# Scores and AV of two tiles of a fused attention and MLP kernel on the diagonal quadrants of TensorE, V kept by parity halves, and the first part of w_in in four transfers

## The chip, the core and the metric

The kernel runs on one core of one Trainium2 chip. The metric is the device time of one execution in microseconds, as the median of several runs. Lower is better. The core's engines are TensorE (PE, with its weight loads shown apart as PEld), VectorE (DVE), ScalarE (ACT), GpSimd (POOL) and SyncE (SP), which here only issues DMA transfers. Each engine works through its own list in order.

## The reference, cut to what matters

```python
q, k, v: (8, 8, 576, 64) float32     # batch, heads, sequence, head dimension
# attention within chunks of 64 keys, no mixing between chunks
scores = 1/8 * q_c @ k_c^T           # per batch, head and chunk: 64 x 64
attn   = softmax(scores)
x      = (attn @ v_c) as (4608, 512) # tokens by heads x head dimension
h      = gelu(x @ w_in)              # w_in: 512 x 2048
out    = h @ w_out                   # w_out: 2048 x 512
```

## The kernel before, in words

**Tiles.** The 4608 tokens are cut into nine tiles of 512 tokens: tile t < 8 holds the first eight chunks of batch t, and tile 8 holds the ninth chunk of all eight batches. Two heads stand together on the 128 partitions, as a pair `g` of four: head 2g on partitions 0 to 63, head 2g+1 on 64 to 127. `CT` = 8 is the number of chunks of a tile, `CH` = 64 their length, `MT` = 512.

**Attention of tiles 0 and 1** (the later seven go another way, by `quad_S` and `quad_av`, which use 64x64 products on all four quadrants of TensorE). Q and K are cast to bf16 and turned by TensorE (`transposed`, L207); `att_Tq` (L213) copies the turned Q, `att_Tk` (L220) the turned K. K's copy goes into `k_bds[g]`, in which each chunk is a 128x128 block with the two heads on its diagonal and zeros beside them. `att_S` (L361 to 369) makes eight products of 128x128 weights by 64 columns for a pair of heads, one for each chunk (L366), and the exponential (L368). V is loaded with 128 keys on the partitions (`load_v`, L181) and cast into `v_bds[i]`, which again holds diagonal blocks (`cast_v`, L201: one piece for each head and parity of the chunk, 64x256 each). `att_av` makes eight products for a pair (L440) and multiplies by the inverse sums into `x` (L442). The zeros beside the diagonals are set by `zero_k` and `zero_v` (L71 to 77) and by two memsets in the main list (L1172).

**The MLP of tile 0** runs while the weights arrive. For each block `f` of 128 of the 2048 hidden columns, four products (one for each part `ks` of the 512) and a GELU (L465 by `by_halves`, called at L481 and L491; L484, L493). `by_halves` cuts a product of 512 columns into two of 256. Blocks 0 and 1 are done first, part by part (`mm1_slices`, L1203). The second layer of tile 0 goes by rows of `w_out` (`mm2_rows`, L1025, f = 0 to 11, four products each), the last four rows by `mm2_slot` (L989).

**What sets the order.** The program is a list written by hand from L1098 on. `phase(0, {...})` at L1204 hangs the attention of tile 1 between the rows of tile 0's second layer: key s of the table names what is issued ahead of row s. So the scores of tile 1's pairs are issued ahead of rows 8, 9, 10 and 11, and its AV products ahead of the later slots 13, 14 and 15 and, for the last pair, in tile 1's first layer (`last_av`).

**Transfers.** SP issues all loads in one list: Q and K of tile 0 in pieces, V of tile 0 (eight transfers, one for each head), `w_in` in four parts of 1 MB (the first three in two transfers each, L1067, of 256 columns; the fourth in one), the four parts of `w_out` (L1075, 1 MB each) with Q and K of tile 1 between them, V of tile 1. Arrivals are in float32 in one of six `arrival` buffers; `win[c](i, engine)` (L1070) and `wout[c](i, engine)` (L1078) cast a block of them to bf16. Row f = 8 of the second layer, L1025, needs the first block of `w_out`'s third part, which POOL casts (L1186).

Of the kernel before, what the change touches and what calls it, by code (L numbers as in the profile page):

```python
# [11 lines left out]
def kernel(  # L12
# [10 lines left out]
    P = 128  # L23
# [46 lines left out]

    def zero_v(i, eng):  # L71
        eng.memset(v_bds[i][0:CH, :, :, CH:P], 0.0)
        eng.memset(v_bds[i][CH:P, :, :, 0:CH], 0.0)

    def zero_k(k_bd, eng):
        eng.memset(k_bd[0:CH, :, CH:P], 0.0)
        eng.memset(k_bd[CH:P, :, 0:CH], 0.0)
# [99 lines left out]
    def load_v(t):  # L177

        tiles[t]["vf"] = stage_tile()[:].rearrange("p (h n d) -> p h n d", h=H, d=D)
        for h in range(H):  # L180
            nc.sync.dma_start(tiles[t]["vf"][:, h], v[t, h, 0:MT, :].rearrange("(n key) d -> key n d", key=P))  # L181
# [16 lines left out]
    def cast_v(t, g, r, copies):  # L198
        to = slice(CH * r, CH * (r + 1))
        for c, copy in enumerate(copies):  # L200
            copy(v_bds[t % NV][to, c:CT:2, g, to], tiles[t]["vf"][CH * c:CH * (c + 1), 2 * g + r])  # L201
# [14 lines left out]
    def att_Tk(t, g, copy):  # L216
        tp = transposed(t, "k", g)
        for r in range(2):
            sl = slice(CH * r, CH * (r + 1))
            copy(k_bds[g][sl, :, sl].rearrange("p i (c j) -> p i c j", j=J), tp[sl])  # L220
# [139 lines left out]

    def att_S(t, g):  # L361
        st = tiles[t]
        pool, tag = (ps_tp, "tp") if t == 1 and g > 1 else (ps_at, "at")
        s_ps = pool.tile([P, CT, CH], f32, tag=tag, name="s_ps")
        for i in range(CT):
            nc.tensor.matmul(s_ps[:, i, :], k_bds[g][:, i, :], st["qT", g][:, i], start=True, stop=True)  # L366
        pT = work.tile([P, CT, CH], bf16, tag="pT", name="pT", bufs=5)
        nc.scalar.activation(pT[:], s_ps[:], Act.Exp, scale=scale)  # L368
        st["pT", g] = pT
# [65 lines left out]
    def att_av(t, g):  # L435
        st = tiles[t]
        pool, tag = (ps_tp, "tp") if t == 1 and g > 1 else (ps_at, "at")
        av_ps = pool.tile([P, CT, CH], f32, tag=tag, name="av_ps")
        for i in range(CT):
            nc.tensor.matmul(av_ps[:, i, :], v_bds[t % NV][:, i, g, :], st["pT", g][:, i, :], start=True, stop=True)  # L440
        x, av, rc = st["x"][:, g, :], av_ps[:].rearrange("p i e -> p (i e)"), st["rc", g][:]
        nc.vector.tensor_tensor(x, av, rc.rearrange("p n e -> p (n e)"), op=mybir.AluOpType.mult)  # L442
# [17 lines left out]
    def by_halves(to, left, right, start, stop):  # L460

        n = to.shape[-1] // 2
        for a in range(2):
            cols = slice(n * a, n * (a + 1))
            nc.tensor.matmul(to[:, cols], left, right[:, cols], start=(start and a == 0), stop=stop, skip_group_check=True)  # L465

    def mm1_slices(t, pools, steps):
# [4 lines left out]
        for step in steps:  # L472
# [3 lines left out]
            for ks in step[1]:  # L476
                for f in step[0]:
                    if ks == 0:
                        pool, tag = pools[f]
                        h_ps[f] = pool.tile([P, MT], f32, tag=tag, name="h_ps")  # L480
                    (nc.tensor.matmul if t else by_halves)(h_ps[f][:], w_in_sb[:, ks, f * P:(f + 1) * P], st["x"][:, ks, :],  # L481
                                                           start=(ks == 0), stop=(ks == KS - 1))
                    if ks == KS - 1:
                        nc.scalar.activation(st["h"][:, f, :], h_ps[f][:], Act.Gelu)  # L484

    def mm1_slot(t, f):
# [3 lines left out]
        for ks in range(KS):  # L490
            (nc.tensor.matmul if t else by_halves)(h_ps[:], w_in_sb[:, ks, f * P:(f + 1) * P], tiles[t]["x"][:, ks, :],  # L491
# [520 lines left out]
    def mm2_rows(t, f):  # L1012
# [8 lines left out]
        for ms, fi in order:  # L1021
# [3 lines left out]
            (by_halves if 2 <= f < 5 else nc.tensor.matmul)(  # L1025
# [71 lines left out]
    with tc.manual_schedule():  # L1097
# [4 lines left out]
        win = [load_w_in(c, 2) for c in range(NWC - 1)]  # L1102
        act_table(Act.Exp)
        keep_warm(7)
        zero_k(k_bds[0], nc.gpsimd)
        zero_k(k_bds[1], nc.gpsimd)
        zero_v(0, nc.vector)
        T, S_, U, A = att_units(0, DV, AC)
        cast_qk(0, "k", 0, PO)
        zero_k(k_bds[2], nc.gpsimd)  # L1110
        cast_qk(0, "k", 1, PO)
        zero_k(k_bds[3], nc.gpsimd)
        cast_qk(0, "k", 2, PO)
        cast_qk(0, "k", 3, PO)
        for g in range(G - 1):
            for r in range(2):
                cast_v(0, g, r, (PO, PO))
        cast_v(0, G - 1, 0, (PO, PO))
        win[0](0, PO)
# [29 lines left out]
        cast_v(0, G - 1, 1, (DV, DV))  # L1149
        A[2]()  # L1150
        win[0](1, AC)
# [4 lines left out]
        win[0](2, DV)  # L1156
# [3 lines left out]
        for c in range(1, NWC):  # L1160
# [8 lines left out]
            if c < 3:  # L1169
                r = slice(CH * (c - 1), CH * c)  # L1170
                o = slice(CH * (2 - c), CH * (3 - c))
                nc.gpsimd.memset(v_bds[1][r, :, :, o], 0.0)  # L1172
# [16 lines left out]
        for g in (0, 2, 3):  # L1189
            for r in range(2):  # L1190
                cast_v(1, g, r, (PO, PO))
# [7 lines left out]
        def sums():  # L1199
# [3 lines left out]
        mm1_slices(0, (mm, mm), (((0, 1), range(KS)),))  # L1203
# [3 lines left out]
                      11: [lambda: wout[3](3, AC), S_[3]], 12: [lambda: cast_v(1, 1, 0, (AC, AC)), lambda: cast_v(1, 1, 1, (AC, AC)), sums],  # L1207
                      13: [A[0], lambda: over[0](2), lambda: over[0](3), U[1]], 14: [A[1], U[2]], 15: [A[2], U[3]]},
              by_rows=True, first=2)
# [158 lines left out]
```

## Time and profile before

| | us |
|---|---|
| median of 3 runs | 267.13 |
| lowest, highest | 266.97, 267.51 |
| the profiled execution | 267.09 |
| its span in the trace | 265.5 |
| PE busy | 256.1 (96% of the span) |
| DVE, ACT, POOL busy | 223.1, 190.5, 103.2 |

The span begins at the first instruction of the program in the trace; 1.6 us of the profiled execution lie around it. All times of places below are from the span's start. The chain of waits is followed back from the last instruction: at each step to what released it, or to the instruction before it on its engine. "PEld" rows are weight loads, which run beside the products. "SPq" is the sequencer of SP, which issues transfers.

### The profile page before, as it was taken

How to read it: one execution, taken by the hardware profiler on the slowest of the kernel's cores; microseconds unless marked ns; L12 is line 12 of the kernel's file. 1: busy time of each engine (PE TensorE's matmuls, PEld its weight loads, DVE VectorE, ACT ScalarE, POOL GpSimd, SP SyncE). 2: the span in 40 equal slices, each digit the busy share in tenths (PEclk: the TensorE clock that was granted, in tenths of full speed). 3: DMA queues.
4: the chain of work that ended last, by engine and by line, in shares of the span. 5: the costliest groups of instructions: out<-in, count | busy, mean ns of one | idle time of the engine just before them, and what ended most of it. 6: DMA issues, size and time to landing. Idle time of an engine off the chain costs nothing.

```text
span 265.5 us, 7854 instructions
## 1 busy us (share of the span) xinstructions
PE 256.1 (96%) x3122; PEld 210.6 (79%) x3122; DVE 223.1 (84%) x394; ACT 190.5 (72%) x386; POOL 103.2 (39%) x225
## 2 busy tenths in 40 slices
PE   6789999999999999999999999999999999999993
PEld 2478875556888888887888888888888888888882
DVE  6874986898897599678999999999999999948772
ACT  3856758987767987898888588947894789227720
POOL 7767778702364291481372095009411300000000
PEclk9999999999999999999999999999999999999998
DMA  6999998999979979999999988998973410130014
GB/s 201 268 311 396 395 401 236 283 193 289 243 195 284 220 175 244 275 239 249 276 245 232 267 186 237 217 175 195 264 160 80 134 42 2 41 119 3 2 40 125
DMA packets 123416, 54.02 MB, mean 203 GB/s; under 512 B 97776, under 2 KB 120304, under 8 KB 123376
## 3 DMA queue, kind: packets, MB, share of 16 engines
q1 hardware_dynamic: 123072, 53.23, 77.4%
q8 instruction: 25, 0.41, 0.7%
q10 hardware_dynamic: 304, 0.26, 0.3%
q14 instruction: 15, 0.12, 0.1%
HBM read 36.70 MB, written 9.44 MB: 174 GB/s over the span
## 4 chain that ended last, share of the span: by engine, by line
PE 76%; DMA 10%; ACT 7%; SPq 4%; issue 1%; DVE 0%; POOL 0%
PE hs_ps L601 31%; PE y_ps L761 22%; PE y_ps L791 13%; DMA arrival<-in_moe_w_out_dram 8%; ACT h L609 3%; SPq L181 2%; PE h_ps L491 2%; DMA arrival<-in_moe_w_in_dram 2%; PE av_ps L349 2%; PE h_ps L481 2%; ACT pT L272 2%; SPq L142 1%; PE y_ps L1025 1%; PE y_ps L989 1%; PE s_ps L264 1%; ACT L1095 1%
## 5 line engine op out<-in xcount | busy, mean ns | idle before, releaser
L609 ACT ACTIVATE h<-hs_ps 128x512 bf16<-128x512 f32 x87 | 49.6, 609 | 6.5 <-PE hs_ps L601 5.7
L238 POOL CAST v_nat<-arrival 128x256 bf16<-128x256 f32 x56 | 24.9, 473 | 33.5 <-DMA arrival<-in_v_dram 23.1
L601 PEld LDWEIGHTS <-w_in_sb 128*128 128x128 bf16 x348 | 33.9, 98 | 4.7 <-issue 0.2
L194 POOL CAST q_nat<-arrival 128x256 bf16<-128x256 f32 x40 | 16.8, 467 | 50.2 <-DMA arrival<-in_k_dram 25.3
L601 PE MATMUL hs_ps<-x,w_in_sb 128*128 128x256 bf16 x232 | 31.8, 272 | 0.0
L761 PEld LDWEIGHTS <-h 128*128 128x128 bf16 x240 | 23.2, 98 | 2.8
L1095 ACT ACT_TABLE_LOAD x16 | 20.5, 1283 | 1.3 <-PEq L1352 1.0
L190 POOL CAST k_nat<-arrival 128x256 bf16<-128x256 f32 (+1 forms) x44 | 19.1, 476 | 5.3 <-DMA arrival<-in_k_dram 5.3
L721 ACT COPY kept<-y_ps 128x512 f32<-128x512 f32 (+1 forms) x17 | 9.0, 536 | 16.0 <-PE y_ps L761 15.9
L761 PE MATMUL y_ps<-w_out_sb,h 128*128 128x256 bf16 x160 | 18.6, 273 | 0.0
L761 PE MATMUL y_ps<-v_bd,k_bd 128*128 128x256 bf16 x160 | 18.5, 273 | 0.1
L761 PEld LDWEIGHTS <-k_bd 128*128 128x128 bf16 x160 | 15.6, 98 | 2.1 <-issue 0.2
L618 ACT COPY hs_ps<-hs_ps 128x512 f32<-128x512 f32 x29 | 16.2, 583 | 0.6 <-PE hs_ps L601 0.5
L601 PE MATMUL hs_ps<-k_bd,w_in_sb 128*128 128x256 bf16 x116 | 16.6, 272 | 0.0
L493 ACT ACTIVATE h<-h_ps 128x512 bf16<-128x512 f32 x21 | 12.5, 604 | 5.5 <-PE h_ps L465 4.1
L272 ACT ACTIVATE pT<-s_ps 128x512 bf16<-128x512 f32 x28 | 14.4, 599 | 1.8 <-PE s_ps L264 1.8
L791 PEld LDWEIGHTS <-h 128*128 128x128 bf16 x144 | 13.8, 98 | 1.7
L465 PE MATMUL h_ps<-x,w_in_sb 128*128 128x256 bf16 x128 | 14.5, 273 | 0.1
L601 PE MATMUL hs_ps<-k_bd,w_in_more 128*128 128x256 bf16 x96 | 14.2, 273 | 0.0
L601 PEld LDWEIGHTS <-w_in_more 128*128 128x128 bf16 x128 | 12.5, 98 | 2.0 <-issue 0.3
L726 DVE TENSOR_TENSOR kept<-y_ps,kept 128x512 f32<-128x512 f32 (+1 forms) x16 | 10.4, 651 | 4.3 <-PE y_ps L761 2.3
L465 PEld LDWEIGHTS <-w_in_sb 128*128 128x128 bf16 x128 | 12.3, 98 | 2.1 <-DVE w_in_sb L1070 0.7
(175 smaller groups left out, 638.9 us busy)
## 6 DMA issues: line engine op xcount, KB each, us to landing
arrival<-in_v_dram SPq DMA_DIRECT2D x58, 128.0 KB, 3.2
arrival<-in_k_dram SPq DMA_DIRECT2D x28, 256.0 KB, 5.6
arrival<-in_q_dram SPq DMA_DIRECT2D x7, 1024.0 KB, 6.9
out_dram<-kept SPq DMA_DIRECT2D x24, 256.0 KB, 3.2
arrival<-in_moe_w_out_dram SPq DMA_DIRECT2D x4, 1024.0 KB, 12.1
arrival<-in_moe_w_in_dram SPq DMA_DIRECT2D x6, 512.0 KB, 8.5
out_dram<-y_sb SPq DMA_DIRECT2D x8, 256.0 KB, 2.5
arrival<-in_v_dram SPq DMA_DIRECT2D x28, 64.0 KB, 2.7
```

The lines of the kernel that those rows point to most:

```text
L190: copy(st[nm][:, q0:q0 + n, g], st[nm + "f"][:, 2 * q0:2 * (q0 + n), g].rearrange("p (q r) d -> p q r d", r=2))
L194: copy(st[nm][:, g, j:j + 2].rearrange("p j r d -> p r j d"), st[nm + "f"][:, 2 * g:2 * g + 2, j:j + 2])
L238: copy(st["v"][:, r::2, n], st["vf"][:, r::2, n])
L272: nc.scalar.activation(pT[:].rearrange("p u (c j) -> p u c j", j=J), tiles[t]["s_ps"][m // 2][m % 2][:].rearrange("p u (j c) -> p u c j", ...
L465: nc.tensor.matmul(to[:, cols], left, right[:, cols], start=(start and a == 0), stop=stop, skip_group_check=True)
L493: nc.scalar.activation(tiles[t]["h"][:, f, :], h_ps[:], Act.Gelu)
L601: nc.tensor.matmul(hs[:, f], left[:, ks, f * P:(f + 1) * P], right[:, ks], start=(fresh and f == 0 and ks == 0), stop=(ks == 1), skip_grou ...
L609: nc.scalar.activation(h[:, n:n + HM, HD * c:HD * (c + 1)], src, Act.Gelu)
L618: "s11": lambda: AC(place_of("b")[:], bank["a"][:]),
L761: nc.tensor.matmul(to, left(f, m), right[:, f], start=(fresh and (split or m == 0) and f == 0), stop=(f == HF - 1), skip_group_check=True)
L791: nc.tensor.matmul(bank[name][:, m], left(f, m), right[:, f], start=(fresh and m == 0 and f == 0), stop=(f == HF - 1), skip_group_check=True)
L1095: nc.scalar.activation(act_scratch[:], rest[:, 0:1], func)
```

## The change

Products: a new helper, `both_halves`, makes the scores and the AV of tiles 0 and 1. For each chunk it issues two products of 64x64 weights by 64 columns, one for the lower half of the partitions and one for the upper half, at the two diagonal quadrants of TensorE. A pair of heads takes 16 products where it took eight.

Operands: K is copied in one piece (128x512) without a diagonal form, V arrives with 64 keys on half of the partitions (head 2g below, head 2g+1 above) and is cast in pieces of 128x256 by POOL, or 128x512 by DVE and ACT. All memsets of zeros go. The turned Q of tile 0's last pair is copied by ACT in place of DVE.

Weights: `w_in`'s first part comes in four transfers of 128 columns (rows of 512 B) in place of two of 256 columns (1 KB).

MLP of tile 0: `by_halves` goes, its products have 512 columns; blocks 0 and 1 are no longer done part by part but one after the other; the four casts of the first part of `w_in` are shared out anew.

```diff
-            nc.sync.dma_start(tiles[t]["vf"][:, h], v[t, h, 0:MT, :].rearrange("(n key) d -> key n d", key=P))
+            r = h % 2
+            nc.sync.dma_start(tiles[t]["vf"][CH * r:CH * (r + 1), h // 2],
+                              v[t, h, 0:MT, :].rearrange("(i key) d -> key i d", key=CH))
...
-        for r in range(2):
-            sl = slice(CH * r, CH * (r + 1))
-            copy(k_bds[g][sl, :, sl].rearrange("p i (c j) -> p i c j", j=J), tp[sl])
+        kT = k_bds[g][:].rearrange("p i c -> p (i c)")[:, 0:MT].rearrange("p (i c) -> p i c", c=CH)
+        copy(kT.rearrange("p i (c j) -> p i c j", j=J), tp)
...
+    def both_halves(to, left, right):
+
+        for i in range(CT):
+            for r in range(2):
+                sl = slice(CH * r, CH * (r + 1))
+                nc.tensor.matmul(to(i)[sl], left(i)[sl], right(i)[sl], start=(i == 0), stop=True,
+                                 tile_position=(CH * r, CH * r), skip_group_check=True)
...
-        for i in range(CT):
-            nc.tensor.matmul(s_ps[:, i, :], k_bds[g][:, i, :], st["qT", g][:, i], start=True, stop=True)
+        both_halves(lambda i: s_ps[:, i, :], lambda i: st["kT", g][:, i], lambda i: st["qT", g][:, i])
...
-        for i in range(CT):
-            nc.tensor.matmul(av_ps[:, i, :], v_bds[t % NV][:, i, g, :], st["pT", g][:, i, :], start=True, stop=True)
+        both_halves(lambda i: av_ps[:, i, :], lambda i: st["vr"][:, g, i, :], lambda i: st["pT", g][:, i, :])
...
-        win = [load_w_in(c, 2) for c in range(NWC - 1)]
+        win = [load_w_in(c, 2 if c else 4) for c in range(NWC - 1)]
...
-        mm1_slices(0, (mm, mm), (((0, 1), range(KS)),))
...
-              by_rows=True, first=2)
+              by_rows=True)
```

PE, at the end of the scores of tile 1's third pair (`s_ps<-s_sb,k_bd_83`, of which the last load and product are shown; `k_bd_83` is K of that pair, `s_sb` holds the turned Q), ahead of the sum over the first pair's exponentials (`sum_ps`) and the next row of tile 0's second layer (`y_ps`). Before:

```order
L366 LDWEIGHTS k_bd_83
L366 MATMUL s_ps<-s_sb,k_bd_83 128x64
L374 LDWEIGHTS ones_bd
L374 MATMUL sum_ps<-pT,ones_bd 128x512
L1025 LDWEIGHTS h
L1025 MATMUL y_ps<-w_out_sb,h 128x512
```

With the change, at the same place:

```order
L361 LDWEIGHTS k_bd_83
L361 MATMUL s_ps<-s_sb,k_bd_83 64x64
L376 LDWEIGHTS ones_bd
L376 MATMUL sum_ps<-pT,ones_bd 128x512
L1019 LDWEIGHTS h
L1019 MATMUL y_ps<-w_out_sb,h 128x512
```

Nothing has moved here; the group has 16 loads and 16 products of 64x64 where it had eight of each over the whole array, and between full products of 128x512 on either side. The same holds for the other scores and for the AV of tile 1 (`av_ps`, L440 before, L361 with the change).

SP, at the start of its list, from the end of Q and K of tile 0 to the first part of `w_out` (the shapes are those of the destinations). Before:

```order
L181 DMA arrival<-in_v_dram 128x4x64 x8
L1067 DMA arrival<-in_moe_w_in_dram 128x4x256 x6
L1067 DMA arrival<-in_moe_w_in_dram 128x4x512
L1075 DMA arrival<-in_moe_w_out_dram 128x4x512
L142 DMA arrival<-in_q_dram 128x8x256
L1075 DMA arrival<-in_moe_w_out_dram 128x4x512
```

With the change:

```order
L175 DMA arrival<-in_v_dram 64x8x64 x8
L1061 DMA arrival<-in_moe_w_in_dram 128x4x128 x4
L1061 DMA arrival<-in_moe_w_in_dram 128x4x256 x4
L1061 DMA arrival<-in_moe_w_in_dram 128x4x512
L1069 DMA arrival<-in_moe_w_out_dram 128x4x512
L134 DMA arrival<-in_q_dram 128x8x256
```

The order of the data is the same; V's eight transfers go to half of the partitions each, and two transfers of `w_in` have become four of half their width.

POOL, from the last casts of K of tile 0 over those of V (`v_bd_79`) and of `w_in` to the first casts of `w_out` and of Q of tile 1 (`v_bd_80` is the home of V of tile 1). Before:

```order
L196 CAST k_nat<-arrival 128x2x4x64 x2
L201 CAST v_bd_79<-arrival 64x4x64 x14
L1070 CAST w_in_sb<-arrival 128x4x128 x4
L1172 MEMSET v_bd_80 64x32x64
L1070 CAST w_in_sb<-arrival 128x4x128 x2
L1172 MEMSET v_bd_80 64x32x64
L1070 CAST w_in_sb<-arrival 128x4x128 x2
L1078 CAST w_out_sb<-arrival 128x512 x2
L196 CAST q_nat<-arrival 128x2x4x64 x3
```

With the change:

```order
L191 CAST k_nat<-arrival 128x2x4x64 x3
L196 CAST v_bd_79<-arrival 128x256 x6
L1064 CAST w_in_sb<-arrival 128x4x128 x8
L1072 CAST w_out_sb<-arrival 128x512 x2
L191 CAST q_nat<-arrival 128x2x4x64 x3
```

Six casts of V take the place of 14, and no memset stands between the casts of the weights any more.

56 lines of the change are left out of this document (18 added, 38 removed).

## The prediction

> **What bounds the kernel now.** First the page: who is busy, and what the chain that ended last is made of.
>
> ```profile
> PE 256.1 (96%) x3122; PEld 210.6 (79%) x3122; DVE 223.1 (84%) x394; ACT 190.5 (72%) x386; POOL 103.2 (39%) x225
> PE 76%; DMA 10%; ACT 7%; SPq 4%; issue 1%; DVE 0%; POOL 0%
> ```
>
> PE is the bound of the whole. The 10% of DMA is one stretch at the start, and the change is made of things in and just behind that stretch. So the next view is the chain in order of time (start, length, what).
>
> ```profile
> 11.87 5.30 DMA arrival<-in_moe_w_in_dram
> 17.19 0.62 ACT w_in_sb L1070
> ...
> 18.78 22.29 DMA arrival<-in_moe_w_out_dram x2
> 41.13 0.62 POOL w_out_sb L1078
> 41.79 1.02 PE y_ps L1025 x4
> 42.82 0.22 PE tp L207 x4
> 43.04 0.23 PE s_ps L366 x8
> 43.27 0.86 PE y_ps L1025 x4
> ...
> 47.84 0.23 PE av_ps L440 x8
> 48.08 0.86 PE y_ps L989 x4
> ```
>
> Up to 41.07 the chain is a transfer: the third part of w_out lands, POOL casts its first block, and row f = 8 of tile 0's second layer starts at 41.79. From there PE follows PE almost without a break to the end. Is the transfer late because it was issued late, or because the DMA engines are full? The windows tell (last three columns: granted clock, DMA share, GB/s).
>
> ```profile
> 10.00:15.00 5.00, 3.48 (x58) 2.19 (x57) 4.80 (x11) 4.91 (x8) 4.19 (x11) 1.00 0.97 227
> 20.00:25.00 5.00, 4.97 (x46) 4.21 (x45) 2.11 (x3) 3.68 (x7) 3.40 (x3) 1.00 1.07 393
> 35.00:40.00 5.00, 5.00 (x49) 3.77 (x48) 3.60 (x6) 2.05 (x5) 3.65 (x5) 1.00 1.06 404
> 40.00:45.00 5.00, 4.68 (x48) 2.67 (x47) 3.13 (x5) 3.92 (x8) 3.87 (x8) 1.00 0.87 237
> ```
>
> The engines are full from 10 to 40 us and let go only after 40. POOL's timeline shows the same from the other side: it stands still for arrivals, at w_in's second part and at w_out's third.
>
> ```profile
> 21.20 0.87 POOL L1070 CAST w_in_sb<-arrival 128x512 bf16<-128x512 f32 x1 [2.05 <-DMA arrival<-in_moe_w_in_dram]
> 41.13 2.29 POOL L1078 CAST w_out_sb<-arrival 128x512 bf16<-128x512 f32 x4 [0.91 <-DMA arrival<-in_moe_w_out_dram]
> ```
>
> So there are two regimes, with the border at 41.79. Ahead of it, work saved on PE, POOL, DVE or ACT is lost again in a wait for the transfer; only the transfers count. Behind it every 0.1 us of PE is 0.1 us of the kernel.
>
> **Ahead of the border: what the engines save.** POOL loses its memsets of zeros and takes six casts of V in place of 14, ACT and DVE copy K once where they copied it in two halves.
>
> ```profile
> 10.86 6.29 POOL L201 CAST v_bd<-arrival 64x256 bf16<-64x256 f32 x14
> L1172 POOL MEMSET v_bd<- 64x2048 bf16 x2 | 3.6, 1797 | 0.1
> L220 ACT COPY k_bd<-tp 64x512 bf16<-64x512 bf16 x12 | 6.9, 578 | 5.9 <-PE tp L207 5.8
> 17.95 3.39 PEld L465 LDWEIGHTS <-w_in_sb 128*128 128x128 bf16 x32
> 21.65 3.39 PEld L465 LDWEIGHTS <-w_in_sb 128*128 128x128 bf16 x32 [0.31 <-DVE w_in_sb L1070]
> 25.42 0.66 PEld L465 LDWEIGHTS <-w_in_sb 128*128 128x128 bf16 x7 [0.38 <-DVE w_in_sb L1070]
> 41.03 0.38 PE L207 MATMUL tp<-ident,k_nat 128*128 128x128 bf16 x4 [0.17 <-ACT k_bd L220]
> ```
>
> This lets tile 0's first layer start before 17.95, by an estimated 0.7 to 1.6 us: V's casts no longer fill POOL until 17.15, and of the 512 KB whose landing let the cast at 17.19 go only half is needed first, 0.7 us at 393 GB/s and 1.3 at 202. But block f = 4 needs w_in's second part, whose arrival ends POOL's 2.05 us of idle time at 21.20 and, on DVE, sets PE's start at 21.65. Four blocks are 3.5 us of PE, so any start ahead of 18.1 is given back there. The gain of the first layer is nothing. Between 21.65 and 41.79 PE may save its waits (0.38 and 0.17 in the rows, and 0.31 ahead of 41.79: the scores that start at 41.25 take 0.23). Halves cost a little more than whole products (0.1092 each by 12.23 us for 112, against 0.2155 for a whole one by 0.86 for four), 0.003 us for each of 48 + 12 products, 0.18. All of it is 1.0 us less PE work ahead of row 8, and row 8 doesn't start sooner, since w_out's landing and cast are not moved by it.
>
> ```profile
> 185.62 12.23 PE hs_ps L601 x112
> 41.25 0.40 PE L366 MATMUL s_ps<-s_sb,k_bd 128*128 128x64 bf16 x8
> ```
>
> That blocks 0 and 1 run one after the other in place of part by part costs nothing for the same reason: the wait at f = 4 covers it.
>
> **Ahead of the border: what the transfers lose.** The bytes are the same. V has as many rows of 256 B as before, and I cost its move to half of the partitions at nothing. But w_in's first part now has 2048 rows of 512 B for 1024 rows of 1 KB. The trace has no 512 B rows; it has 256 B alone (10.2 to 13 us), 1 KB alone (19.2 to 22) and nearly alone 2 KB (24 to 27): packets, MB, share of 16 engines.
>
> ```profile
> q1 hardware_dynamic: 2274, 0.56, 89.1%
> ...
> q1 hardware_dynamic: 1053, 1.05, 106.6%
> ...
> q1 hardware_dynamic: 623, 1.22, 105.1%
> ```
>
> Time of one packet on its engine: 0.891 x 16 x 2.8 us / 2274 = 17.6 ns, 1.066 x 16 x 2.8 / 1053 = 45.4 ns, 1.051 x 16 x 3 / 623 = 81 ns. These three lie on a line (the first two would put 2 KB at 82), so 512 B should take 27 ns, a third of the way: 2048 x 27 / 16 = 3.5 us against 1024 x 45.4 / 16 = 2.9. **The stream behind it is 0.6 us late.** The bounds are a packet that costs as one of 256 B (-0.7) and one that costs as one of 1 KB (+2.9); I take the line. SP issues two more transfers, which the full engines hide. The later stream moves row 8 from 41.79 to 42.4. PE would be there at about 41.6 (21.65 + 0.6 + 20.14 - 0.86 - 0.18, and 0.23 more for the first pair's scores), so the wait for w_out grows and swallows what PE saved.
>
> The Trainium skill has a rule that speaks for the four transfers: "DMA: Bandwidth & Descriptors", Specifications, gives 512 B as the least transfer at line rate. By that the stream would lose nothing. The trace shows no 512 B row, and its 1 KB rows at 373 GB/s against 408 at 2 KB show that a row of 1 KB isn't at the full rate yet.
>
> **Behind the border: the quadrant groups.** From 41.79 on PE has seven of the eight groups of tile 1 (scores of three pairs, AV of four; the first pair's scores lie ahead of row 8). Each is 0.23 us now: eight products, the weight loads hidden. The new ones use 64x64 quadrants, which the kernel's later tiles use already, four at a time.
>
> ```profile
> 46.17 0.38 PE L1025 MATMUL y_ps<-w_out_sb,h 128*128 128x512 bf16 x1
> 46.48 0.40 PE L392 MATMUL sums_ps<-pT,ones_c 128*32 128x512 bf16 x4
> 46.81 0.39 PE L989 MATMUL y_ps<-w_out_sb,h 128*128 128x512 bf16 x1
> ...
> 71.93 0.49 PE L761 MATMUL y_ps<-v_bd,k_bd 128*128 128x256 bf16 x3
> 72.35 0.74 PE L349 MATMUL av_ps<-pT,v_nat 64*64 64x64 bf16 x64
> 73.02 0.28 PE L761 MATMUL y_ps<-v_bd,k_bd 128*128 128x256 bf16 x1
> ```
>
> A whole product of 512 columns is followed by the next after 0.2155 us. Ahead of the four products on strips of 32 columns (128*32) PE takes 0.31, behind them 0.33 though they run side by side: about 0.09 to go into another division of the array and 0.1 to come out. The 64 quadrant products agree: the third full product of the row starts at 72.15 and would be followed at 72.26, the first quadrant product comes at 72.35, the next full one at 73.02. That is 0.76 in all, less 0.2 for the two changes 0.56, and 16 rounds of four products at 0.035. A quadrant thus takes a new load and product every 0.035 us. The new group has eight rounds of two: 0.2 + 8 x 0.034 = **0.46 against 0.23**. Fewer quadrants in a round cannot shorten it below eight products of 64 columns in a row, 8 x 0.027 (256 columns take 0.109) = 0.22, so the group is 0.42 at least; at most the two quadrants don't overlap at all, 16 x 0.029 + 0.2 = 0.66. I take the nearest row: 0.23 more for each, seven groups, **1.6 us**. Nothing covers them, since PE follows PE there and no later wait of the chain is for a transfer. On PE's list the second layer's rows stand behind each group, and all the rest behind these.
>
> **Sum.** 0.6 (transfers, by the line) + 1.6 (seven groups) + 0 (first layer) = 2.2 us. The profiled execution took 267.09, so 269.3; it stands 0.04 below the median of the runs shown, which changes nothing.
>
> **The rivals.**
>
> *The 512 B rows cost nothing* (the skill's figure, or stalls at the start of w_in that have nothing to do with size). Then row 8 stays at 41.79 and only the groups count: 267.09 + 1.6 = 268.7. For it: w_in's first half took 5.3 us from issue to landing while V was still moving, so something else than packets slows it. Against: the line through three sizes.
>
> *The pairs of quadrants don't run side by side*, so that the change doesn't do what it says: 0.66 for a group, seven times 0.43 more, 267.09 + 0.6 + 3.0 = 270.7. For it: two products of one quadrant now stand two apart on PE's list, where quadrants had four apart. Against: each quadrant gets its next load and product within 0.035 us in the 64-product row. The Trainium skill, "TensorE: Matmul & The Clock Gate", Part 3, "The mechanism", would lead there too: it lets a weight load overlap only products of another row group, so a quadrant's own load would lie open ahead of its product. By that rule the rows of four at 0.035 couldn't be, as two loads and two products of each row group lie in them; I give it little.
>
> *The front is not bound by transfers* (the other side). The landings follow the engine that comes last; the full engines on average may be well ahead of it. If what holds that engine up falls at another place now, w_out's third part lands earlier and PE's savings count. Price: the first layer up to 1.6 earlier, its waits and halves 1.0, the first scores 0.2 back, 2.4 in all; with the seven groups 267.09 - 2.4 + 1.6 = 266.3. It decides from the point at which row 8 starts before 40.2 (41.79 - 1.6), for which the landing must come before 39.5. For it: POOL, DVE and ACT have more air, and the 0.31 at 21.65 and 0.38 at 25.42 are partly waits for casts. Against: the engines' share of 1.06 from 20 to 40 us, and 0.91 us in which POOL stood ready for w_out and nothing came.
>
> **How the numbers follow.** Chances: the forecast 54% (268.9 to 269.9 by itself), free 512 B rows 18%, no overlap of the pairs 7%, the front freed 12%, and 5% for a part of it that cancels against the groups (266.6 to 267.6, no change). The last 4% are packets of 512 B towards their upper bound, 271 to 272. The predicted time is 269.3. The range leaves out the freed front and its part below and those 4% above: 267.6 to 270.9. A measurement of this kernel can tell about 0.2% (0.5 us) from no change. Faster by more: 11%, nearly all of the freed front; within: 6%; slower: 83%.
>
> **What would show it.** In the changed kernel's chain, the groups of tile 1 (`s_ps`, `av_ps`) should take 0.4 to 0.5 us each with the switches, which show as PE starting 0.09 late into them and 0.1 late out of them. The 512 B packets should average about 27 ns. Tile 0's first layer should start before 17.4 and then wait at block 4 for more than a microsecond. Row 8 should start at 42.2 to 42.6, behind a POOL cast that waited for w_out. From there to the end it should be 1.6 us longer than now. Wrong would be: row 8 before 41.5 (then the front wasn't bound by the stream as I think), or groups below 0.3 (then the switch is not paid by two quadrants), or a new wait behind row 8, for V's casts or K's copies, that no term has.

## The result, and the profile after

The changed kernel takes 270.71 us (median of 17 runs, 269.49 to 272.23) where the kernel before took 267.13 (17 runs beside it). The ratio is 1.0136, 95% interval 1.011 to 1.0162: it is slower by 3.6 us, with an interval of 2.9 to 4.3. The forecast was 2.2 slower. In the experiments below, two runs more than 1.5% above the fastest of their kernel are left out of the ratios, 274.33 us of a_two_transfers and 274.99 of a_warm_wait; without them the medians of these two are 270.15 and 270.70.

The page of the changed kernel, the same two lines as before. TensorE is busy for longer (260.0 us for 256.1, a part of it at half the clock, as is seen below), and the transfers' share of the chain has gone from 10% to 3%.

```profile
PE 260.0 (96%) x3174; PEld 204.7 (76%) x3174; DVE 216.3 (80%) x388; ACT 186.9 (69%) x378; POOL 91.6 (34%) x201
PE 83%; ACT 6%; SPq 5%; DMA 3%; issue 1%; DVE 0%
```

The chain in order of time (start, length, what). This profiled execution took 272.09, span 270.5, so it is one of the longer ones; the span before was 265.5.

```profile
12.67 1.67 SPq L1061
15.50 8.15 DMA arrival<-in_moe_w_in_dram
24.16 11.86 PE h_ps L485 x48
...
44.85 0.97 PE y_ps L1019 x4
```

The last transfer in the chain is now w_in's second part, which lets block f = 4 start at 24.16, not w_out's third part. From 24.16 PE follows PE. The first row of the chain is new too: SP stood 1.67 us at one issue of w_in, from 12.67 on. TensorE's timeline around tile 0's first layer (start, length, idle time ahead and its releaser):

```profile
17.11 0.82 PE L485 MATMUL h_ps<-x,w_in_sb 128*128 128x512 bf16 x3
18.17 2.10 PE L485 MATMUL h_ps<-x,w_in_sb 128*128 128x512 bf16 x9 [0.23 <-DVE x L443]
20.53 1.04 PE L485 MATMUL h_ps<-x,w_in_sb 128*128 128x512 bf16 x4 [0.26 <-POOL w_in_sb L1064]
24.16 3.01 PE L485 MATMUL h_ps<-x,w_in_sb 128*128 128x512 bf16 x7 [2.59 <-DVE w_in_sb L1064]
```

As forecast, the layer starts early (17.11) and gives it back at block 4. But it gives back too much: block 4 starts at 24.16 where it started at 21.65. And seven products behind the wait take 3.01 us, 0.43 each, at half the clock. The windows (granted clock, DMA share, GB/s at the end of each row) show the stream:

```profile
10.00:15.00 5.00, 3.92 (x97) 2.96 (x99) 4.34 (x10) 4.37 (x8) 2.85 (x7) 1.00 0.91 213
20.00:25.00 5.00, 2.15 (x9) 0.60 (x8) 0.44 (x2) 1.23 (x3) 1.34 (x2) 0.85 1.06 363
35.00:40.00 5.00, 5.00 (x34) 2.64 (x33) 3.47 (x7) 3.74 (x6) 3.98 (x5) 1.00 1.07 398
40.00:45.00 5.00, 5.00 (x52) 2.87 (x50) 3.16 (x4) 2.14 (x4) 2.77 (x5) 1.00 1.01 321
```

From 10 to 15 us the engines are less full (0.91 for 0.97), and from 40 to 45 they still move 321 GB/s where they had let go (237). POOL's two waits for transfers come about 2.5 us later than at 21.20 and 41.13:

```profile
23.70 0.87 POOL L1064 CAST w_in_sb<-arrival 128x512 bf16<-128x512 f32 x1 [3.23 <-DMA arrival<-in_moe_w_in_dram]
43.65 2.29 POOL L1072 CAST w_out_sb<-arrival 128x512 bf16<-128x512 f32 x4 [1.45 <-DMA arrival<-in_moe_w_out_dram]
```

Behind the border, TensorE's timeline of the changed kernel: row 8, then K's turn, the scores of a pair, row 9, and at the end the first layer of tile 1 behind the last AV.

```profile
44.78 1.04 PE L1019 MATMUL y_ps<-w_out_sb,h 128*128 128x512 bf16 x4
45.66 0.39 PE L202 MATMUL tp<-ident,k_nat 128*128 128x128 bf16 x4
45.98 0.44 PE L361 MATMUL s_ps<-s_sb,k_bd 64*64 64x64 bf16 x16
46.35 1.04 PE L1019 MATMUL y_ps<-w_out_sb,h 128*128 128x512 bf16 x4
...
56.54 3.84 PE L475 MATMUL h_ps<-x,w_in_sb 128*128 128x512 bf16 x17
```

The same end in the kernel before:

```profile
51.85 3.83 PE L481 MATMUL h_ps<-x,w_in_sb 128*128 128x512 bf16 x17
```

From row 8 to there it is 56.54 - 44.78 = 11.76 us, and was 51.85 - 41.79 = 10.06: 1.70 more, against 1.6 forecast. So this execution divides into 2.99 us ahead of row 8 (41.79 to 44.78), 1.70 in the groups, and 0.3 further on; together 5.0, the difference of the two spans. The front is where the forecast was short.

### The profile page after: what moved, and what is told of

It is laid out like the page before. It is cut to its first block, busy times and chain, and to the rows that moved or that the text cites. A ratio compares the mean times of both kernels' runs of the same rounds, so it can differ in the third digit from the quotient of the medians.

```text
span 270.5 us, 7923 instructions
## 1 busy us (share of the span) xinstructions
PE 260.0 (96%) x3174; PEld 204.7 (76%) x3174; DVE 216.3 (80%) x388; ACT 186.9 (69%) x378; POOL 91.6 (34%) x201
## 4 chain that ended last, share of the span: by engine, by line
PE 83%; ACT 6%; SPq 5%; DMA 3%; issue 1%; DVE 0%
PE hs_ps L595 30%; PE y_ps L755 22%; PE y_ps L785 13%; PE h_ps L485 7%; PE y_ps L1019 4%; DMA arrival<-in_moe_w_in_dram 3%; ACT h L603 3%; SPq L175 2%; PE av_ps L344 2%; PE h_ps L475 2%; ACT pT L267 1%; PE y_ps L983 1%; SPq L134 1%; SPq L1061 1%; PE s_ps L259 1%; ACT L1089 1%
## 5 line engine op out<-in xcount | busy, mean ns | idle before, releaser
L603 ACT ACTIVATE h<-hs_ps 128x512 bf16<-128x512 f32 x87 | 49.7, 612 | 7.2 <-PE hs_ps L595 6.2
L233 POOL CAST v_nat<-arrival 128x256 bf16<-128x256 f32 x56 | 27.8, 519 | 32.4 <-DMA arrival<-in_v_dram 31.6
L595 PEld LDWEIGHTS <-w_in_sb 128*128 128x128 bf16 x348 | 33.9, 98 | 4.7 <-issue 0.2
L189 POOL CAST q_nat<-arrival 128x256 bf16<-128x256 f32 x40 | 15.8, 441 | 54.9 <-DMA arrival<-in_q_dram 37.2
L485 PE MATMUL h_ps<-x,w_in_sb 128*128 128x512 bf16 x92 | 22.7, 397 | 3.1 <-DVE w_in_sb L1064 2.6
L487 ACT ACTIVATE h<-h_ps 128x512 bf16<-128x512 f32 x23 | 13.7, 604 | 10.0 <-PE h_ps L485 9.9
L485 PEld LDWEIGHTS <-w_in_sb 128*128 128x128 bf16 x92 | 9.1, 101 | 14.6 <-DVE w_in_sb L1064 3.1
L595 PE MATMUL hs_ps<-k_bd,w_in_more 128*128 128x256 bf16 x96 | 14.2, 273 | 0.0
L599 DVE TENSOR_TENSOR hs_ps<-hs_ps,kept_p 128x512 f32<-128x512 f32 x15 | 10.3, 690 | 4.9 <-PE hs_ps L595 4.4
## 6 DMA issues: line engine op xcount, KB each, us to landing
arrival<-in_moe_w_out_dram SPq DMA_DIRECT2D x4, 1024.0 KB, 12.6
```

The costliest lines, as they stand in the source:

```text
L189: copy(st[nm][:, g, j:j + 2].rearrange("p j r d -> p r j d"), st[nm + "f"][:, 2 * g:2 * g + 2, j:j + 2])
L233: copy(st["v"][:, r::2, n], st["vf"][:, r::2, n])
L485: nc.tensor.matmul(h_ps[:], w_in_sb[:, ks, f * P:(f + 1) * P], tiles[t]["x"][:, ks, :], start=(ks == 0), stop=(ks == KS - 1))
L487: nc.scalar.activation(tiles[t]["h"][:, f, :], h_ps[:], Act.Gelu)
L595: nc.tensor.matmul(hs[:, f], left[:, ks, f * P:(f + 1) * P], right[:, ks], start=(fresh and f == 0 and ks == 0), stop=(ks == 1), skip_grou ...
L603: nc.scalar.activation(h[:, n:n + HM, HD * c:HD * (c + 1)], src, Act.Gelu)
```

## The experiments

All times are medians. Each ratio, with its interval, is to the kernel before on the same chip (266.8 to 267.1 us). It is not the ratio of the medians and can differ from it, most in b_four_transfers, whose median stands 0.7 us above that of the kernel before while the ratio shows no difference. Differences in us are worked out from the ratios. "Row 8" is its start in that kernel's one profiled execution, "cast" the start of POOL's cast of w_out's third part, "fetch" the start of the first packet of the kind "instruction" with 16 KB. Names that begin with a_ are the changed kernel with something undone, those with b_ the kernel before with something added.

| kernel | us | ratio, 95% interval | fetch | cast | row 8 |
|---|---|---|---|---|---|
| before | 267.13 | 1 | 19.03 | 41.13 | 41.79 |
| changed | 270.71 | 1.0136, 1.011 to 1.0162 | 12.67 | 43.65 | 44.78 |
| a_two_transfers | 270.30 | 1.0107, 1.006 to 1.0153 | 14.03 | 44.47 | 45.16 |
| b_four_transfers | 267.50 | 0.9999, 0.9968 to 1.003 | 17.03 | 40.24 | 42.01 |
| a_warm_wait | 270.99 | 1.0122, 1.0073 to 1.017 | 14.18 | 43.06 | 43.73 |
| b_v_on_halves | 267.35 | 1.0016, 0.9991 to 1.0041 | 17.66 | 40.62 | 41.29 |
| b_more_rows | 268.48 | 1.0051, 1.0029 to 1.0074 | 12.83 | 42.08 | 42.75 |
| b_whole_mlp | 268.00 | 1.0035, 1.0006 to 1.0065 | 18.61 | 40.24 | 41.36 |
| b_tile1_quadrants | 269.21 | 1.0082, 1.0055 to 1.0109 | 18.75 | 40.92 | 41.59 |
| a_tile1_whole | 271.31 | 1.0171, 1.0136 to 1.0207 | 11.94 | 42.23 | 44.85 |
| a_tile0_whole | 270.16 | 1.0109, 1.0064 to 1.0155 | 16.49 | 42.08 | 42.75 |
| a_tile1_whole_2 | 269.14 | 1.0089, 1.0059 to 1.0119 | 12.91 | 42.04 | 42.89 |
| b_rows_first | 268.89 | 1.0077, 1.0049 to 1.0104 | 6.59 | 39.94 | 41.07 |

Four theories for the front stood at the start: T1 the 512 B rows, T2 V's way onto half of the partitions, T3 TensorE's clock, T4 the fetch of TensorE's own code.

### a_two_transfers and b_four_transfers: the 512 B rows

```diff
 # a_two_transfers, on the changed kernel
-        win = [load_w_in(c, 2 if c else 4) for c in range(NWC - 1)]
+        win = [load_w_in(c, 2) for c in range(NWC - 1)]
 # b_four_transfers, on the kernel before: the other way round
```

> The changed kernel, with w_in's first part in two transfers again (1024 rows of 1 KB in place of 2048 of 512 B). Four theories for the front of the changed kernel, in which w_in's second part lands 2.5 us later than before (23.65 against 21.14): T1, the 512 B rows cost 0.6 us of the stream: the second part lands near 23.0 and the time falls by 0.6, to about 270.1. T2, V's way onto half of the partitions holds the stream up: nothing changes, 270.7. T3, the chip halves TensorE's clock after its wait at block 4: the wait gets 0.6 shorter at most, 270.1 to 270.7. T4, the earlier instruction fetch of TensorE at 12.67 us holds up one DMA engine: nothing changes, 270.7.

> The kernel before, with w_in's first part in four transfers (2048 rows of 512 B). T1 (512 B rows cost 0.6): the second part of w_in lands near 21.7 in place of 21.14, row 8 of tile 0's second layer starts near 42.4 and the time is 267.1 + 0.6 = 267.7. T2 to T4: nothing, 267.1. If a row of 512 B went at the full rate: 267.1 as well.

Undoing the four transfers gains nothing that can be told (+2.9 us on the kernel before, 1.6 to 4.1, where the changed kernel has +3.6, 2.9 to 4.3). Making them in the kernel before costs nothing that can be told: -0.03 us, between -0.9 and +0.8. The times alone leave room for T1's 0.6, so the traces have to decide. The DMA view from 14 to 16 us, first b_four_transfers with rows of 512 B, then the kernel before with rows of 1 KB (packets, MB; then the queue's packets, MB and share of 16 engines):

```profile
DMA packets 1241, 0.62 MB, mean 308 GB/s; under 512 B 40, under 2 KB 1241, under 8 KB 1241
q1 hardware_dynamic: 1241, 0.62, 108.3%
```

```profile
DMA packets 590, 0.59 MB, mean 296 GB/s; under 512 B 12, under 2 KB 590, under 8 KB 590
q1 hardware_dynamic: 590, 0.59, 100.9%
```

A packet of 512 B takes 1.083 x 16 x 2 us / 1241 = 27.9 ns, close to what the line through three sizes gave. But a packet of 1 KB takes 1.009 x 16 x 2 / 590 = 54.7 ns at this place, not the 45.4 of 19 to 22 us. Three more kernels with 1 KB rows here (b_whole_mlp, b_tile1_quadrants, b_rows_first) show 48.9 to 49.7 ns in the same two microseconds, a few rows of 256 B included. So two packets of 512 B, 55.8 ns, cost 1 to 7 ns more than one of 1 KB, and 1024 such pairs on 16 engines come to 0.1 to 0.4 us, less than T1's 0.6. The stream as a whole was not late either: POOL took w_out's third part at 40.24, 0.9 us before the kernel before did. So the 512 B rows are not what makes the front late by 2 us. The Trainium skill, "DMA: Bandwidth & Descriptors", Specifications, gives 512 B as the least transfer for line rate. The trace agrees in that little is lost against 1 KB here, but 308 GB/s at this place is not the 408 of 2 KB rows later.

Row 8 of b_four_transfers started only at 42.01, 1.77 us behind the cast. TensorE itself was late there: its granted clock was 0.57 from 14 to 16 us and 0.58 from 16 to 18.

### a_warm_wait: TensorE's clock

```diff
+        if t == 0 and f == 4:
+            for _ in range(10):
+                nc.tensor.matmul(h_ps[:], rest[:, 0:P], rest[:], start=True, stop=True)
         for ks in range(KS):
```

> The changed kernel with ten whole products of 512 columns put ahead of block 4 of tile 0's first layer (into the same PSUM tile, which the block then overwrites), so that TensorE works for about 2.2 of the 2.75 us in which it now waits for w_in. T3 (the clock falls to 0.50 for 3.4 us because TensorE stood still): the clock stays at 1.00 from 22 to 28 us, the seven products that took 0.427 each take 0.216, and the time falls by up to 1.3, to 269.4 to 270.0. T1, T2, T4 alone: the wait is for the transfer, the time stays at 270.7.

The windows from 22 to 26 us, the changed kernel first, then this one (granted clock third from the end):

```profile
22.00:24.00 2.00, 0.00 (x0) 0.00 (x0) 0.33 (x1) 0.20 (x1) 0.29 (x1) 0.86 1.08 374
24.00:26.00 2.00, 1.84 (x5) 0.74 (x6) 0.53 (x2) 0.00 (x0) 1.44 (x2) 0.50 1.07 402
```

```profile
22.00:24.00 2.00, 2.00 (x11) 0.90 (x10) 0.43 (x1) 0.68 (x2) 0.72 (x1) 1.00 1.04 340
24.00:26.00 2.00, 2.00 (x11) 0.87 (x9) 0.43 (x1) 0.60 (x1) 1.02 (x2) 1.00 1.07 387
```

The clock stayed at 1.00, as T3 said, and the time did not fall in a way that can be told (+3.3 us on the kernel before, 1.9 to 4.5, where the changed kernel has +3.6). The trace shows why it gained little: row 8 came at 43.73, right behind the cast of w_out at 43.06, so the saved clock ended in the wait that the prediction had named. In the changed kernel's own profile TensorE is just behind this wait (cast 43.65, row 8 at 44.78, 1.13 apart where 0.67 is usual when row 8 waits for it), so the half clock cost at most 0.5 us there. It is a follower of the late stream, not the cause.

### b_v_on_halves: V's transfers

```diff
+        if t == 0:
+            tiles[t]["vf"] = stage_tile()[:].rearrange("p (g i d) -> p g i d", g=G, d=D)
+            for h in range(H):
+                r = h % 2
+                nc.sync.dma_start(tiles[t]["vf"][CH * r:CH * (r + 1), h // 2],
+                                  v[t, h, 0:MT, :].rearrange("(i key) d -> key i d", key=CH))
+            return
```

> The kernel before, with tile 0's V fetched as the changed kernel does, each transfer onto 64 of the partitions, and cast from there to the diagonal form; its products stay whole. T2 (V on half of the partitions holds up the stream; in the changed kernel SP took 0.63 to 0.75 us for each issue where it took 0.51): V's last landing moves from 14.16 to near 15.4, w_in's second part from 21.14 to 22 to 23, and the time is 268 to 269. T1, T3, T4: nothing, 267.1.

The time is +0.4 us, between -0.2 and +1.1: not told from nothing. POOL took w_in's second part at 20.71, earlier than the 21.20 of the kernel before, so T2's chain of events didn't come about in this execution. The mechanism is half there. SP took 0.63 us for each of the last issues of V where it took 0.51, and the share of the DMA engines from 11 to 13 us (40 slices of 0.05 us, in tenths) falls to 1 around 11.2 and to 3 around 12.1. This kernel first, then the kernel before:

```profile
DMA  2111111336778999999654343456799999898889
```

```profile
DMA  7899999988888867875687987889999999778999
```

### b_more_rows: the fetch of TensorE's code

```diff
+    def tiny(n):
+        warm = ps_mm.tile([P, MT], f32, tag="mm", name="warm")
+        for _ in range(n):
+            nc.tensor.matmul(warm[:, 0:2], rest[:, 0:P], rest[:, 0:2], start=True, stop=True)
...
         T[1]()
+        tiny(16)
         keep_warm(3)
 # and tiny(16) at three more places among tile 0's scores
```

> The kernel before, with 64 products of 2 columns (and their 64 weight loads) strewn among the scores of tile 0, as many instructions of TensorE as the changed kernel has more for tile 0's attention. TensorE has idle time there. T4 (the early instruction fetch of TensorE, which takes 16 KB over one DMA engine for 1 us while the other engines still move V in rows of 256 B, holds up the stream): the first fetch comes at 12.5 to 15 us in place of 17 to 19, w_in's second part lands 1 to 2.5 us later than 21.14, row 8 starts at 42.8 to 44.3, and the time is 268 to 269.5. If the fetch does no harm: 267.1.

The time is as T4 expected: +1.4 us (0.8 to 2.0), with no other part of the change in it. The way there is so only in part: the fetch came early (12.83), but w_in's second part was not late (POOL took it at 20.87, and at 21.20 in the kernel before), and row 8 at 42.75 is just short of the expected range. TensorE's code comes in packets of 16 KB (queue q8, kind "instruction"). That the queue is TensorE's shows in its count: 25 packets for 3122 loads and 3122 products in the kernel before, 26 for 3174 and 3174 in the changed one. The first came when TensorE had begun 209 loads and products here; in the kernel before it came at 19.03. The row of its queue from 12 to 13 us, the chain's row of SP, and POOL's wait for w_out:

```profile
q8 instruction: 1, 0.02, 6.0%
```

```profile
12.85 1.36 SPq L1067
```

```profile
42.08 2.29 POOL L1078 CAST w_out_sb<-arrival 128x512 bf16<-128x512 f32 x4 [1.20 <-DMA arrival<-in_moe_w_out_dram]
```

6% of 16 engines for 1 us is one engine for 0.96 us. SP stands at the issue that it began at that moment, for 1.36 us in place of 0.51, and the third part of w_out is cast 0.95 us later. (A long issue is no mark of a fetch by itself: in the kernel before SP stood 1.60 us at one from 14.07 on, with no such packet under way.) In the changed kernel the fetch at 12.67 and SP's 1.67 us at 12.67 are the same pair of events. What the other engines do meanwhile is seen in the share of the engines from 12.6 to 14 us, first the changed kernel, then b_four_transfers, which has no fetch there:

```profile
DMA  9998766465554446799998878943433234564676
```

```profile
DMA  6979999999999989969795869798999999999999
```

From 13.5 us on the engines of the changed kernel are 2 to 7 tenths busy, as if they ran out of what SP has issued. The table goes the same way over all kernels: where the first fetch came between 11.9 and 16.5 us, w_out's third part was cast at 42.04 or later; where it came at 6.6 or from 17 us on, at 41.13 or earlier. (In a_tile1_whole POOL was still casting K, so its 42.23 doesn't tell the landing.)

This doesn't single the fetch out, though. Of the seven kernels with a fetch between 11.9 and 16.5 us all but this one also have V on half of the partitions. And in some of them less had come already before the fetch. The windows from 10 to 12 us, the kernel before first, then b_more_rows (GB/s at the end):

```profile
10.00:12.00 2.00, 1.48 (x21) 0.82 (x18) 1.93 (x4) 1.96 (x4) 1.58 (x4) 1.00 0.90 202
```

```profile
10.00:12.00 2.00, 1.72 (x23) 1.06 (x22) 1.94 (x4) 1.49 (x4) 1.76 (x4) 1.00 0.74 170
```

In the same window a_two_transfers has 138 and a_warm_wait 96 GB/s, and their fetches came at 14.03 and 14.18. Of the 1.5 us by which the span of b_more_rows is longer in its trace, 0.96 lie ahead of row 8. So that added instructions cost time is shown; that they do it by the fetch is likely, and not shown.

### b_tile1_quadrants: the groups alone

```diff
+        if t == 1:
+            both_halves(lambda i: s_ps[:, i, :], lambda i: st["kT", g][:, i], lambda i: st["qT", g][:, i])
+        for i in range(CT) if t == 0 else ():
             nc.tensor.matmul(s_ps[:, i, :], k_bds[g][:, i, :], st["qT", g][:, i], start=True, stop=True)
 # the same for the AV; V and K of tile 1 as in the changed kernel, without the two memsets of L1172
```

> The kernel before, with the scores and the AV of tile 1 alone on quadrants; tile 0, V of tile 0 and w_in stay. Only the term of the seven groups is in it: each 0.46 in place of 0.23, so 267.1 + 1.6 = 268.7, with row 8 at 41.8 as before. If the whole loss of 3.6 were behind row 8: 270.7.

The time is +2.2 us, between 1.5 and 2.9, around the 1.6 of the forecast. Row 8 and the end of the groups in its timeline:

```profile
41.59 1.02 PE L1055 MATMUL y_ps<-w_out_sb,h 128*128 128x512 bf16 x4 [0.53 <-POOL w_out_sb L1108]
...
53.33 3.84 PE L511 MATMUL h_ps<-x,w_in_sb 128*128 128x512 bf16 x17
```

53.33 - 41.59 = 11.74, which is 1.68 more than before: the term is real and stands by itself, and row 8 still waits for w_out.

### a_tile1_whole and a_tile1_whole_2: the front alone

```diff
 # a_tile1_whole: tile 1's scores and AV over diagonal forms again, the zeros set by POOL
+        for i in range(G):
+            zero_k(k_bds[i], nc.gpsimd)
         for i in range(FC):
             wout[0](i, DV if i % 2 == 0 else PO)
 # a_tile1_whole_2: the same zeros behind V's and w_in's first casts
```

> The changed kernel, with the scores and the AV of tile 1 whole again: tile 0 on quadrants, V of tile 0 on halves, w_in's first part in four transfers. It keeps what the changed kernel does to the front and drops the seven groups: 270.7 - 1.6 = 269.1, row 8 still near 44. If nothing but the groups cost time: 267.1.

The first try got slower (271.31), by a wait that the experiment made itself. Eight memsets of 0.5 to 0.8 us stood ahead of POOL's casts of w_out's first part, and TensorE waited for these:

```profile
36.47 1.24 PE L1044 MATMUL y_ps<-w_out_sb,h 128*128 128x512 bf16 x5 [2.51 <-POOL w_out_sb L1097]
```

So its time tells nothing of the groups, though its trace does: from row 8 (44.85) to the end of the groups it is 10.07 us, as in the kernel before. The second try puts the zeros where POOL has time:

> The changed kernel with tile 1 whole again, once more, with its memsets of zeros now at places where POOL stands idle (behind the casts of V and of w_in's first part), since in the first try they stood ahead of the casts of w_out and TensorE waited 2.7 us for POOL. Only the front of the change is in it: 270.7 - 1.6 = 269.1, with TensorE waiting for no cast of POOL behind 30 us. If the groups cost nothing: 270.7.

269.14, +2.4 us (1.6 to 3.2), as expected, and the groups are back to their old length:

```profile
42.89 1.03 PE L1044 MATMUL y_ps<-w_out_sb,h 128*128 128x512 bf16 x4
...
52.95 3.83 PE L500 MATMUL h_ps<-x,w_in_sb 128*128 128x512 bf16 x17
```

52.95 - 42.89 = 10.06. So what the change does besides the groups costs 2.4 us, the groups 1.7 by the traces, and the sum of 4.1 lies within the measured 2.9 to 4.3. (With the 2.2 that b_tile1_quadrants has by its time the sum would be 4.6; the intervals are too wide to tell.) The trace is that of the fastest run, 268.43: row 8 comes 1.10 us later than in the kernel before, where it came 2.99 later in the changed kernel's long one. So the price of the front changes from one execution to the next, and the 2.4 rests on ten of them.

### a_tile0_whole: the rest of the front

```diff
 # b_tile1_quadrants, and besides:
-        win = [load_w_in(c, 2) for c in range(NWC - 1)]
+        win = [load_w_in(c, 2 if c else 4) for c in range(NWC - 1)]
-        mm1_slices(0, (mm, mm), (((0, 1), range(KS)),))
...
-              by_rows=True, first=2)
+              by_rows=True)
 # by_halves gone, tile 0's V onto half of the partitions as in b_v_on_halves
```

> Like the changed kernel, but tile 0's scores and AV stay whole products over diagonal forms (with their memsets and casts of V as before); V of tile 0 on halves, w_in's first part in four transfers, the whole MLP products and tile 1 on quadrants are kept. T4 (128 instructions of TensorE more on tile 0 bring its first fetch forward into the time in which V moves): the first fetch comes at 17 us or later, the third part of w_out lands near 40.5 to 41 as in the kernels without those instructions, and only the groups of tile 1 are left: 267.1 + 1.6 = 268.7. If the rest of the front (V, w_in, MLP) is what costs: 270.7.

T4 alone fails here: 270.16 is +2.9 us (1.7 to 4.1), nearer to the 270.7 of the other answer than to its 268.7. Without the additional instructions the front is still late in the trace (cast at 42.08). Its fetch came at 16.49, earlier than expected, and was a long one; SP stood 2.86 us beside it. The queue's row from 16.4 to 19 us and the chain's row:

```profile
q8 instruction: 1, 0.02, 5.3%
```

```profile
16.39 2.86 SPq L1102
```

5.3% of 16 engines for 2.6 us is 2.2 us for one packet. So either a fetch can also hurt behind V, or the late front has another cause here; no run tells which. What moves the fetch is more than the number of instructions: TensorE had begun 247 loads and products here, 209 to 231 in the other kernels with a fetch between 11.9 and 16.5 us, 240 to 327 in those with a later one.

### b_rows_first: the fetch at another time

```diff
-        keep_warm(7)
+        tiny(96)
+        keep_warm(1)
```

> The kernel before, with 96 products of 2 columns in place of six of the seven products that TensorE does before its first input arrives. TensorE has 180 instructions more, but its first fetch moves to 5 to 7 us, when Q and K come in rows of 1 KB, and the second to about 17 us, when V has landed. T4 (a fetch hurts only while V's rows of 256 B move): the stream is not late, the third part of w_out lands near 41 and the time is 267.1, within 0.5. If more instructions cost time wherever they stand: 268.5 as with 64 products among the scores, or more.

Half of this held. The fetch came at 6.59, and the front was not late but early: w_out's third part was cast at 39.94, 1.2 us before that of the kernel before, and row 8 started at 41.07. Yet the time is +2.0 us (1.3 to 2.8). POOL's timeline shows where a good part of it went, at V of a later tile:

```profile
97.33 3.02 POOL L238 CAST v_nat<-arrival 128x256 bf16<-128x256 f32 x7
101.79 0.40 POOL L238 CAST v_nat<-arrival 128x256 bf16<-128x256 f32 x1 [1.44 <-DMA arrival<-in_v_dram]
```

TensorE stood 1.1 us for this cast, and 0.3 at 130. The kernel before waits for transfers at neither place. A fetch of 1.74 us began at 98.8 in this execution; whether it held up V's last piece no run shows. The kernel before has one of 1.68 us at 95.5 without such a wait, and b_four_transfers, with no instruction added, has the wait as well in its trace (its longest run, 268.59):

```profile
102.29 0.40 POOL L238 CAST v_nat<-arrival 128x256 bf16<-128x256 f32 x1 [0.60 <-DMA arrival<-in_v_dram]
```

### b_whole_mlp: the MLP of tile 0

```diff
-            (nc.tensor.matmul if t else by_halves)(h_ps[:], w_in_sb[:, ks, f * P:(f + 1) * P], tiles[t]["x"][:, ks, :],
+            nc.tensor.matmul(h_ps[:], w_in_sb[:, ks, f * P:(f + 1) * P], tiles[t]["x"][:, ks, :],
...
-        mm1_slices(0, (mm, mm), (((0, 1), range(KS)),))
```

> The kernel before, with the changed kernel's MLP of tile 0: products of 512 columns in place of two halves, blocks 0 and 1 one after the other. By the prediction row 8 waits for w_out and all savings ahead of it are covered: 267.1. A rival: the halves' instructions are gone, so that the second instruction fetch comes later, and TensorE waits at block 4 where it worked before; if the clock falls in that wait, row 8 comes up to 1 us later, 267.1 to 268.1.

+0.9 us (0.2 to 1.7), and not in the way that the rival meant: the clock stayed at 1.00, and row 8 started 0.4 earlier (41.36). In its profile the time is lost at 130 us, where the turned K of a later tile is late:

```profile
130.34 0.71 PE L264 MATMUL s_ps<-q_t,k_t 64*64 64x64 bf16 x64 [1.14 <-DMA k_t<-k_nat]
```

None of the kernels is faster than the kernel before, so there was no better version to run.

## Why the prediction was right, and where it was short

**What bounds the kernel: right.** The two regimes are there. Work saved on TensorE ahead of row 8 is lost again (the start at 17.11 in the wait at block 4, the clock of a_warm_wait in the wait for w_out), and work added behind it counts in full. But TensorE is never far behind the transfer: in the changed kernel, b_four_transfers, b_whole_mlp and b_rows_first row 8 came 1.1 to 1.8 us behind the cast, where 0.67 is usual, so TensorE's own work set it there.

**The groups: right.** 0.23 more for each of seven was forecast, 1.6 us; the traces of the five kernels with tile 1 on quadrants show 1.67 to 1.70, and those of a_tile1_whole and a_tile1_whole_2, without them, none. The rival that let the pairs run one after the other (0.66 for a group, and the rule of the Trainium skill, "TensorE: Matmul & The Clock Gate", Part 3, "The mechanism", as the forecast read it) is refuted for this form: the group runs from 45.98 to 46.35 with its way in ahead of it, 0.46 in all, so a quadrant's next load does not wait for its own product.

**The first layer: right.** It started before 17.4 and waited at block 4 for 2.6 us.

**The transfers: the step that failed.** "The stream behind it is 0.6 us late" was the term, and it measures about 2: 2.4 (1.6 to 3.2) by a_tile1_whole_2, and 3.6 less the groups' 1.7 = 1.9 by the changed kernel itself. Its working was wrong as well. The 27 ns for a packet of 512 B were right, but they were set against 45.4 ns for 1 KB from a later window; at the place where w_in's first part moves, 1 KB took 49 to 55, so the smaller rows can cost 0.4 us at most. The rival "the 512 B rows cost nothing" was nearly right on this point, and its 268.7 was still wrong, because the front was late for another reason. What the sum lacked is a cost of instructions as such: the 128 loads and products that tile 0 has more have no term in it, and 64 products of two columns with their loads, alone, cost 1.4 us (0.8 to 2.0). How they cost it is argued and not shown. They bring TensorE's next 16 KB of code forward from 19.03 to 12.67 us, where SP then stands at an issue and the DMA engines run dry. But a_tile0_whole has a late front without these instructions, and b_rows_first is 2.0 us slower with a fetch that did its front no harm.

**The number: in part luck.** 270.71 lies within the range of 267.6 to 270.9 by 0.2 us, with 1.4 of the 3.6 missing from the forecast, all but 0.1 of it in the one term whose reason was wrong. It stands next to the 270.7 of the rival without overlap only by chance, since the traces refute that rival's groups.

**V's move at nothing: not settled.** SP takes 0.12 us longer for each issue that nothing else holds up, and the time by itself is -0.2 to +1.1. a_tile0_whole leaves 2.9 less 1.7 = 1.2 us (0 to 2.4) for V, the four transfers and the whole products together. How the front's 2.4 divides between these and the fetch stays open, since the intervals are wider than the parts. So does what kept the later tiles' transfers late in b_rows_first and b_whole_mlp.

**The front not bound by transfers: refuted.** Row 8 came later, not before 40.2. The forecast's picture of it (a start at 42.2 to 42.6 behind POOL's cast) holds in the kernels in which TensorE was in time, at other numbers: 43.73 behind a cast at 43.06 in a_warm_wait.

## What to carry to other kernels

Count what a change adds in instructions on each engine, not only in their time: 64 tiny products cost 1.4 us here. Look for where the code is fetched, since its packets go over the same DMA engines as the data; a fetch in a stretch of short rows, where little is queued ahead, is the likely reason here. Take the price of a packet from the stretch in which it will move, since the same 1 KB took 49 to 55 ns early and 45.4 later. A small group on another division of the array pays its way in and out, here 0.2 of 0.46 us, so make such groups long or keep them off a path that TensorE bounds.

## What the runs showed of the hardware that was not expected

- A packet of 16 KB of kind "instruction" took one DMA engine for 0.88 to 0.97 us in about half of the cases, and 2.2 us at most. In the six kernels whose first one came between 11.9 and 14.2 us, the issue that SP began within 0.15 us of it took 1.3 to 1.8 us, where the issue ahead of it had taken 0.5 to 0.6.
- SP's issue of 128 KB in rows of 256 B took 0.51 us onto 128 partitions and 0.63 us onto 64, where nothing else held it up.
- Behind 2.6 us in which TensorE stood still, the granted clock was 0.50 for about 3.4 us, and a product of 512 columns took 0.43 us in place of 0.2155; ten products in that wait kept it at 1.00. The Trainium skill, "TensorE: Matmul & The Clock Gate", Part 1, "What's actually happening", names a window of 3.4 us for such a gate, which agrees in length. Standing still does not decide alone: in a_tile1_whole TensorE stood 2.5 us ahead of 36.47 and the clock stayed at 1.00, and in b_four_transfers the clock was 0.57 from 14 to 16 us though no wait from 8 us on had reached 0.6.
